# A chunked attention and a feed-forward block on one core: one list of calls, written in another order

## The chip, the core and the metric

The kernel runs on one core of a Trainium2 chip. Its time is the device time in microseconds of one execution. Five engines with instruction streams of their own take part: TensorE (PE; the loads of its weights are shown apart as PEld), VectorE (DVE), ScalarE (ACT), GpSimd (POOL) and SyncE (SP), which only issues transfers. The profile is one execution, recorded by the hardware profiler. An entry such as L388 names line 388 of the kernel's file, often a line inside a helper that is called from many places.

## The reference

First comes a causal linear attention with a decay per head, computed in blocks with a running state, then a feed-forward block on its output, token by token.

```python
# q, k, v: (B, H, S, D) = (4, 8, 768, 64), lam: one decay per head
Dmask = np.where(rel >= 0, lam[:, None, None] ** rel[None, :, :], 0.0)
for b in range(nb):
    intra = einsum('bhic,bhjc->bhij', qb, kb) * Dmask[None]
    intra = einsum('bhij,bhjd->bhid', intra, vb)
    inter = einsum('bhid,bhde->bhie', qb * lam_pow[None], kv_state)
    out[:, :, sl] = intra + inter
    kv_state = lam_block * kv_state + einsum('bhsd,bhse->bhde', kb * rev_pow, vb)
# x: the attention's output as 3072 tokens of 512; w_in: 512 x 2048, w_out: 2048 x 512
h = x @ w_in
g = np.maximum(h, 0.0) + alpha * np.minimum(h, 0.0)
return (g @ w_out).astype(np.float32)
```

The reference takes the attention in blocks of 64 rows. The kernel takes blocks of 128, which gives the same values with another mask and another power of the decay.

## The kernel before

**Units and chunks.** The 3072 tokens are six chunks of 512: chunk c holds the rows of sequence block c // 2 (256 rows) of two of the four batches. The attention of a chunk is four units, one per batch and half of the heads, 24 units in all, numbered n = 0 to 23. A unit has two score blocks of 128 rows for each of its four heads.

**Steps of a unit.** `load` brings q and k as fp32 (SyncE's queue, or GpSimd's with "G"), `load_v16` brings v and casts it to fp16 on the way (GpSimd's queue). `cast` (L245 to L251) makes q and k fp16, on ScalarE ("A"), VectorE ("V") or GpSimd ("G"); this letter stands behind many calls and means the same each time. `turn` transposes them on TensorE (L316) and `turn_copy` takes the result out of PSUM (L249 on VectorE, L247 on ScalarE); `turned` (L303) has a transfer do both. `decayed` multiplies q with its decay (L341). `score_products` (L377) makes the 128 x 1024 scores of a unit in PSUM, in the one buffer `s` that all units share. `masked` (L388, VectorE) multiplies them with the decay mask and frees that buffer. `inter` (L361) and `intra` (L402) add up the output, `attended` copies it to the chunk's `xT`. `key_decayed` (L290 on ScalarE in eight rows, otherwise L292) and `state_products` or `state_in` make the state's update, `states` (L457) and `first_state` write the new state `R`. The masks are made once at the start: `mask_logs` (L195, VectorE) writes the logarithms of the decay for two heads, `decay_mask` (L206, ScalarE) takes their exponential. `tick` (L145) runs products on TensorE whose result nobody reads.

**Steps of the feed-forward block.** `up` (L498) is h = x @ w_in for one of 16 blocks of 128 hidden columns. `relu` (L511, ScalarE) and `prelu` (L526, VectorE) make g from it. `down` and `down_copy` (L534, L548) are the second product of chunk 0 and its way out. `load_win` and `load_wout` bring the weights in four quarters each, cast by GpSimd's queue; `gate` (L115) makes SyncE's queue wait until a quarter is there.

**Seven products for eight.** The second product of chunks 1 to 5 runs as seven products of half the size in place of eight, on sums of weights (`w_sum`) and of values (`g_sum`): `second(c, i, b)` at L655 is one pass of eight products, `last` (L697) the seventh kind for chunk 5. The first product of chunks 4 and 5 is made together in the same manner (`in_sum`, `x_sum`, `first`, L780). All these sums are on VectorE or, with "G", on GpSimd, where L573 is a difference and L576 a sum. `g_sum(c, i, j, k)` overwrites quarters of chunk c's values for i = 2, 3 and 4, so that i = 4 needs i = 2 of the same j and k, which needs i = 1:

```python
if i == 1:
    add(s1, a21, a22, eng)
elif i == 3:
    sub(a21, a11, a21, eng)
elif i == 2:
    sub(a11, s1, a11, eng)
else:
    sub(a12, a12, a11, eng)
```

The pass with i = 5 reads the sum of i = 1, the pass with i = 6 that of i = 2, the pass with i = 7 the difference of i = 3, and the pass with i = 3 (`last` for chunk 5) that of i = 4; the passes with i = 1, 2 and 4 read values that are not yet, or not at all, overwritten.

**What sets the order.** The kernel runs under a manual schedule: each engine executes its instructions in the order in which the program lists the calls. From line 799 on the body is one list of some 1,080 calls, written out. Pools fix how far work can run ahead: four PSUM banks for transposes, projections and outputs, one score buffer, three `m` and three output buffers, five raw buffers for q and k.

**Ordered waits.** `vector_turn(n)` remembers the VectorE instruction listed last, and `gpsimd_waits(n)` makes the GpSimd instruction listed last wait until that one is done (L560, L563). No data passes between the two; the wait only says who goes first.

Of the kernel before, what the change touches and what calls it, by code (L numbers as in the profile page):

```python
# [11 lines left out]
def kernel(  # L12
# [469 lines left out]
    G = {}  # L482
# [315 lines left out]

    load(0, 1, "k", 0, "G")
    query_decay(3, 1)  # L800
    query_decay(2, 1)
    mask_logs(2)
    tick(6)
    load(0, 1, "q", 0, "G")
    mask_logs(0)
    key_decay()
    state_decay()
    load(0, 0, "k", None)
    cast(0, "k16", "V")
    query_decay(0, 1)  # L810
    load(0, 0, "q", None)
    key_decayed(0, "V")
    mask_logs(1)
    key_decayed(1, "V")
    decay_mask(2)
    decay_mask(0)
    cast(1, "k16", "V")
    tick(56)
    load(0, 1, "q", 1, "G")
    load_v16(1)  # L820
    decay_mask(1)
    cast(1, "q16", "A")
    mask_logs(3)
    query_decay(1, 1)
    cast(0, "q16", "V")
    vector_turn(0)
    turn(1, (1,))
    turn_copy(1, (1,), "V")
    decay_mask(3)
    query_decay(0, 0)  # L830
    load_alpha()
    load(0, 1, "k", 1, "G")
    load_v16(0)
    turn(1, (0,))
    turn_copy(1, (0,), "V")
    load_v16(2)
    turn(0, (1,))
    turn_copy(0, (1,), "V")
    turn(0, (0,))
    turn_copy(0, (0,), "A")  # L840
    load_v16(3)
    load_win(1)
    slopes_turn()
    slopes()
    load_win(0)
    decayed(1, "P")
    cast(2, "q16", "A")
    score_products(1)
    masked(1)
    fill(3)  # L850
    key_decayed(2)
    gpsimd_waits(0)
    cast(2, "k16", "A")
    cast(3, "q16", "G")
    gpsimd_waits(0)
    turn(2, (0,))
    turn_copy(2, (0,), "V")
    state_in(1, 0)
    first_state(1)
    decayed(2)  # L860
    decayed(0, "V")
    load_win(3)
    score_products(0)
    key_decayed(3)
    cast(3, "k16", "A")
    turn(2, (1,))
    load(1, 0, "k", 0, "G")
    inter(1)
    turn(3, (0,))
    state_in(0, 0)  # L870
    turn_copy(2, (1,), "A")
    first_state(0)
    intra(1)
    turn(3, (1,))
    attended(1, "A")
    masked(0)
    score_products(2)
    state_in(0, 1)
    inter(0)
    turn_copy(3, (0,), "V")  # L880
    decayed(3)
# [12 lines left out]
    first_state(3)
    masked(3)
    intra(2)
    state_in(3, 1)
    up(0, 4, 0)
    attended(2, "A")
    relu(0, 4, 0)  # L900
    state_in(2, 1)
    states(2, (1,))
    load_win(2)
    states(3, (1,))
    load(1, 1, "q", 1, "G")
    load(1, 0, "k", 1, "G")
    load(1, 0, "q", 1, "G")
    inter(3)
    prelu_half(0, 4, 0)
    intra(3)  # L910
    state_in(1, 1)
    attended(3, "A")
    up(0, 6)
    load_wout(0)
    up(0, 3)
    relu(0, 6)
    relu(0, 3)
    up(0, 5)
    states(1, (1,))
    cast(4, "q16", "G")  # L920
    prelu(0, 6)
    load(1, 1, "k", 1, "G")
    relu(0, 5)
    up(0, 7)
    relu(0, 7)
    load_wout(1)
    prelu(0, 3)
    cast(4, "k16", "G")
    up(0, 13)
    up(0, 15)  # L930
    load_v16(5)
    prelu(0, 5)
    relu(0, 13)
    prelu(0, 7)
    key_decayed(4)
    prelu(0, 13)
    cast(5, "k16", "G")
    cast(5, "q16", "G")
    up(0, 14)
    up(0, 1)  # L940
    relu(0, 15)
    prelu(0, 15)
    turn(4, (0,))
    load(1, 1, "q", 0, "G")
    load_wout(2)
    relu(0, 14)
    relu(0, 1)
    up(0, 0)
    prelu(0, 14)
    turn_copy(4, (0,), "V")  # L950
    up(0, 10)
    relu(0, 0)
    prelu(0, 1)
    turn(4, (1,))
    up(0, 2)
    cast(7, "q16", "A")
    prelu(0, 0)
    relu(0, 10)
    w_sum(1, 1, "G")
    in_sum(1, 2, "G")  # L960
    up(0, 9)
    turn_copy(4, (1,), "A")
    prelu(0, 10)
    up(0, 4, 1)
    relu(0, 2)
    gate(2, "out")
    up(0, 11)
    score_products(4)
    decayed(4, "V")
    query_decay(1, 0)  # L970
    relu(0, 9)
    load(1, 1, "k", 0)
    prelu(0, 2)
    relu(0, 4, 1)
    relu(0, 11)
    load_wout(3)
    state_products(4, None, True)
    prelu(0, 9)
    turn(5, (0,))
    up(0, 8)  # L980
    prelu_half(0, 4, 1)
    turn(7, (0,))
    prelu(0, 11)
    turn(5, (1,))
    turn_copy(5, (0,), "A")
    turn_copy(7, (0,), "V")
    load_v16(7)
    first_state(4)
    turn_copy(5, (1,), "A")
# [919 lines left out]
```

## Time and profile before

| | before |
|---|---|
| runs, us | 201.75, 205.83, 201.48 |
| median, us | 201.75 |
| profiled execution, us | 202.65 |
| its span, us | 200.9 |
| instructions | 5880 |
| TensorE busy, us (share) | 194.7 (97%) |
| VectorE busy, us (share) | 172.7 (86%) |
| ScalarE busy, us (share) | 135.6 (68%) |
| GpSimd busy, us (share) | 142.8 (71%) |
| moved by DMA | 30.53 MB |

The span runs from the first to the last instruction that the profile holds. The profiled execution took 1.75 us more than its span and 0.90 more than the median of the three runs. The ends of TensorE's products are modelled, so a row's end can lie past the start of the next; its starts are the safer reading. The page cuts the span into 40 slices and gives TensorE's granted clock in tenths of full speed, which is 9 ("90% or more") in all of them.

```profile
PE   7999999999999999999999999999999999999992
DVE  6998879987799998999998997999999999996600
ACT  5786778928886897787786692836768877632131
POOL 8999689997999749999799959967520505525300
PEclk9999999999999999999999999999999999999999
```

TensorE is full from the second slice to the last but one. VectorE comes near it in many slices between. GpSimd is full early and has holes from slice 28 on, which is where the first products of chunks 4 and 5 begin.

### The profile page before, as it was taken

The page shows a single profiled execution, that of the slowest core. Times are in us where ns is not written, and L with a number is a line of the kernel's source. Part 1 is how long each engine was busy: PE and PEld are TensorE (multiplying, and loading weights), DVE is VectorE, ACT ScalarE, POOL GpSimd, SP SyncE. Part 2 cuts the span into 40 slices and gives each one's busy share as a digit, 9 for nine tenths or more (in the row PEclk, how much of TensorE's full clock was granted, in tenths as well). Part 3 has the DMA queues.
Part 4 walks back from the last instruction along what each step waited for, and adds up shares of the span by engine and source line. Part 5 has one row for each costly group of instructions (what it writes and reads, how often), then busy time and mean ns, then how long its engine had stood idle before and what let it go on. Part 6 is the DMA issues. An engine that isn't in the chain of part 4 may idle for free.

```text
span 200.9 us, 5880 instructions
## 1 busy us (share of the span) xinstructions
PE 194.7 (97%) x2351; PEld 131.1 (65%) x2351; DVE 172.7 (86%) x319; ACT 135.6 (68%) x303; POOL 142.8 (71%) x161
## 2 busy tenths in 40 slices
PE   7999999999999999999999999999999999999992
PEld 7976445546545688665556777667666556788891
DVE  6998879987799998999998997999999999996600
ACT  5786778928886897787786692836768877632131
POOL 8999689997999749999799959967520505525300
PEclk9999999999999999999999999999999999999999
DMA  5999999999999699999999964011100003002343
GB/s 159 286 193 217 254 264 237 201 261 288 223 226 221 108 235 227 224 236 191 135 202 196 211 177 104 3 57 52 52 0 3 30 24 104 6 0 77 135 144 117
DMA packets 59199, 30.53 MB, mean 152 GB/s; under 512 B 29652, under 2 KB 57956, under 8 KB 59172
## 3 DMA queue, kind: packets, MB, share of 16 engines
q1 hardware_dynamic: 41236, 19.87, 42.6%
q0 software_dynamic: 17776, 10.23, 35.9%
q8 instruction: 18, 0.29, 0.6%
q14 instruction: 9, 0.07, 0.2%
q10 hardware_dynamic: 160, 0.07, 0.1%
HBM read 27.27 MB, written 6.29 MB: 167 GB/s over the span
## 4 chain that ended last, share of the span: by engine, by line
PE 58%; DMA 16%; POOL 10%; DVE 7%; issue 3%; ACT 3%; ACTq 0%; POOLq 0%
PE y L655 13%; PE h_ps L498 11%; PE b L655 10%; DMA v<-in_v_dram 7%; PE b L780 5%; DMA w_out_sb<-in_moe_w_out_dram 5%; DMA w_in_sb<-in_moe_w_in_dram 4%; PE e L780 3%; PE a L780 3%; POOL qdT L341 3%; PE o_ps L534 3%; PE unread L145 3%; DVE g L526 2%; POOL v L272 2%; DVE sm L388 2%
## 5 line engine op out<-in xcount | busy, mean ns | idle before, releaser
L498 PE MATMUL h_ps<-xT,w_in_sb 128*128 128x512 f16 (+1 forms) x264 | 59.5, 373 | 0.4 <-DMA w_in_sb<-in_moe_w_in_dram 0.3
L655 PEld LDWEIGHTS <-g 128*128 128x128 f16 x464 | 44.9, 98 | 10.4 <-issue 0.5
L526 DVE SCALAR_TENSOR_TENSOR g<-m,oma,h_ps 128x512 f16<-128x512 f32 (+1 forms) x66 | 46.2, 727 | 5.4 <-ACT m L511 4.2
L511 ACT ACTIVATE m<-h_ps 128x512 f32<-128x512 f32 (+1 forms) x66 | 37.8, 583 | 12.0 <-PE h_ps L498 11.4
L498 PEld LDWEIGHTS <-w_in_sb 128*128 128x128 f16 x264 | 24.4, 97 | 25.9 <-DMA w_in_sb<-in_moe_w_in_dram 1.0
L388 DVE TENSOR_TENSOR sm<-s,dmask 128x1024 f16<-128x1024 f32 x24 | 29.2, 1218 | 1.1 <-PE s L377 0.8
L655 PE MATMUL y<-w_out_sb,g 128*128 128x256 f16 x224 | 27.6, 273 | 0.2 <-DVE y L576 0.2
L341 POOL TENSOR_TENSOR qdT<-qkT,qdecay 128x512 f16<-128x512 f16 (+1 forms) x20 | 21.1, 1058 | 0.1
L290 ACT ACTIVATE kdec<-kraw,kdecay 128x64 f16<-128x64 f32 x80 | 20.1, 341 | 0.0
L247 ACT ACTIVATE xT<-acc 128x512 f16<-128x512 f32 x21 | 12.6, 598 | 11.0 <-DVE R L457 4.7
L655 PE MATMUL b<-t,g 128*128 128x256 f16 x160 | 19.3, 273 | 0.0
L573 POOL TENSOR_TENSOR g<-g,g 128x512 f16<-128x512 f16 x13 | 14.9, 1166 | 6.2 <-PE y L655 6.2
L272 POOL DMA_DIRECT2D v<-in_v_dram x24 | 18.8, 786 | 0.0
L457 DVE SCALAR_TENSOR_TENSOR R<-R,rdecay,acc 128x128 f16<-128x128 f16 x54 | 15.5, 341 | 1.0 <-ACT xT L247 0.4
L534 PE MATMUL o_ps<-w_out_sb,g 128*128 128x512 f16 x64 | 15.4, 380 | 0.0
L573 POOL TENSOR_TENSOR g<-g 128x512 f16<-128x512 f16 x8 | 9.2, 1155 | 8.6 <-DVE s L576 8.5
L292 POOL TENSOR_TENSOR kdec<-kraw,kdecay 128x512 f16<-128x512 f32 x12 | 12.7, 1057 | 0.2
L573 POOL TENSOR_TENSOR g<-s,g 128x512 f16<-128x512 f16 x5 | 6.1, 1225 | 5.8 <-DVE g L573 4.8
L377 PE MATMUL s<-qkT 64*64 64x128 f16 x384 | 9.9, 220 | 0.3 <-DVE qkT L249 0.2
L247 ACT ACTIVATE o_sb<-y 128x512 f32<-128x512 f32 (+2 forms) x12 | 6.3, 524 | 5.5 <-DMA out_dram<-o_sb 2.3
L576 POOL TENSOR_TENSOR w_in_sb<-g,g 128x512 f16<-128x512 f16 x3 | 3.5, 1159 | 9.1 <-PE a L780 9.1
L247 ACT ACTIVATE qk<-qraw 128x512 f16<-128x512 f32 x14 | 8.7, 625 | 1.7 <-DMA qraw<-in_q_dram 1.7
(131 smaller groups left out, 381.8 us busy)
## 6 DMA issues: line engine op xcount, KB each, us to landing
out_dram<-o_sb SPq DMA_DIRECT2D x23, 256.0 KB, 2.4
kraw<-in_k_dram SPq DMA_DIRECT2D x7, 512.0 KB, 5.6
qraw<-in_q_dram SPq DMA_DIRECT2D x6, 512.0 KB, 5.6
v<-in_v_dram POOLq DMA_DIRECT2D x24, 128.0 KB, 6.0
w_in_sb<-in_moe_w_in_dram POOLq DMA_DIRECT2D x4, 512.0 KB, 8.9
w_out_sb<-in_moe_w_out_dram POOLq DMA_DIRECT2D x4, 512.0 KB, 8.8
qraw<-in_q_dram POOLq DMA_DIRECT2D x6, 256.0 KB, 6.8
qraw<-in_q_dram SPq DMA_DIRECT2D x6, 256.0 KB, 6.0
```

The costliest lines, as they stand in the source:

```text
L247: nc.scalar.activation(out, in_, AF.Copy)
L272: nc.gpsimd.dma_start(out=v16.rearrange("p h e d -> p h (e d)"), in_=v[2 * (c % 2) + bi, ds(4 * hh, 4), ds((c // 2) * W, W), :].rearrange( ...
L290: nc.scalar.activation(kdec[:, e, h], kr[:, e, h], AF.Copy, scale=kdecay[:, x, e : e + 1])
L341: engine(eng).tensor_tensor(out=qdT[:, :, :, p], in0=(t["qps"] if eng == "P" else t["qkT"][:, 0])[:, :, :, p], in1=qdecay[:, hh, :, :, p], ...
L388: nc.vector.tensor_tensor(out=t["sm"].rearrange("p a h x j -> p (a h) x j"), in0=t["s"].rearrange("p a h x j -> p (a h) x j"), in1=mask_of ...
L498: nc.tensor.matmul(h[:, 0:n] if bi is None else h[:, 0:n].rearrange("p (e j) -> p e j", e=2), lhsT=w_in_sb[:, gi, ts(f, 128)], rhs=x.rearr ...
L511: nc.scalar.activation(m[:, 0:n], HP[c, f, bi][:, 0:n], AF.Relu, scale=-1.0)
L526: engine(eng).scalar_tensor_tensor(out=g, in0=m, scalar=oma[:, f : f + 1], in1=h, op0=ALU.mult, op1=ALU.add)
L534: nc.tensor.matmul(O[c, t], lhsT=g_of(c, f)[:, t // 2, t % 2, :], rhs=w_out_sb[:, f, :], start=(f == 0), stop=(f == NF - 1),)
L573: engine(eng).tensor_tensor(out=out, in0=a, in1=b, op=ALU.subtract)
L655: nc.tensor.matmul(Y[c, k][:, ds(b * HALF, HALF)], lhsT=left(c, i, f, b), rhs=right(i, f), start=(f == 0 and b == 0 and i in (1, 5)), stop ...
L780: nc.tensor.matmul(t, lhsT=w, rhs=x, start=(g == 0 and i in (1, 5)), stop=(g == 1), skip_group_check=True)
```

## The change

Nothing before line 799 is changed, and the helpers are the same to the letter. The list of calls from there on is written in another order, and some calls have another engine's letter. TensorE gets the same instructions, and the same transfers are issued. These counts of calls differ:

| call | before | after |
|---|---|---|
| `cast` of q or k on ScalarE, GpSimd, VectorE | 24, 18, 6 | 28, 17, 3 |
| `decayed` on GpSimd, on VectorE | 20, 4 | 23, 1 |
| `turn_copy` on ScalarE, on VectorE | 8, 9 | 5, 12 |
| `key_decayed` on ScalarE, VectorE, GpSimd | 10, 2, 12 | 9, 3, 12 |
| `g_sum` on GpSimd, on VectorE | 37, 43 | 43, 37 |
| `w_sum` on GpSimd, on VectorE | 7, 9 | 9, 7 |
| `vector_turn` | 13 | 16 |
| `gpsimd_waits` | 24 | 21 |

`tick(6)` and `tick(56)` both stood ahead of the first transposes; now `tick(56)` stands there and `tick(6)` behind them. The first loads of q and k on GpSimd's queue come in another order, and six such half blocks of chunk 1 stand ahead of w_out's first quarter, where five stood. `gate(2, "out")`, behind which SyncE's loads of later q and k wait, keeps its place in SyncE's queue. Of the last two chunks' 32 value sums GpSimd makes 20, before 12. The diff is nearly the whole list; this is its start, and its end from the last PReLU on.

```diff
--- before.py
+++ after.py
@@ -796,1082 +796,1082 @@
...
+    key_decay()
+    query_decay(1, 1)
+    load(0, 0, "k", None)
+    mask_logs(3)
+    tick(56)
+    mask_logs(1)
+    cast(0, "k16", "A")
+    cast(1, "k16", "A")
+    load(0, 1, "q", 0, "G")
+    load(0, 1, "q", 1, "G")
+    decay_mask(3)
+    mask_logs(2)
+    turn(0, (1,))
+    load_v16(1)
+    query_decay(3, 1)
+    key_decayed(0, "V")
     load(0, 1, "k", 0, "G")
-    query_decay(3, 1)
+    decay_mask(2)
+    turn(1, (1,))
+    load_v16(0)
+    turn_copy(0, (1,), "V")
+    load_v16(2)
+    load(0, 1, "k", 1, "G")
...
     prelu(5, 15)
-    g_sum(4, 3, 1, 0, "G")
-    second(4, 2, 0)
-    second_b(5)
-    second(4, 2, 1)
-    g_sum(4, 2, 0, 0)
-    second(4, 5, 0)
-    g_sum(5, 1, 1, 1)
-    g_sum(5, 1, 0, 1, "G")
-    second_store(3, 2)
-    second(4, 5, 1)
+    g_sum(4, 2, 0, 1)
+    g_sum(5, 1, 1, 1, "G")
     second(5, 2, 0)
+    second(5, 2, 1)
+    second_out(4, 2)
+    g_sum(4, 3, 1, 1)
+    vector_turn(11)
+    second_store(4, 2)
     second(5, 5, 0)
-    g_sum(5, 3, 1, 1)
-    g_sum(4, 2, 0, 1)
-    second_m5(4)
-    second(5, 5, 1)
-    g_sum(4, 2, 1, 0)
-    g_sum(5, 3, 0, 0)
-    g_sum(4, 3, 1, 1)
-    g_sum(5, 2, 1, 0)
-    second(5, 2, 1)
-    second_m5(5)
-    g_sum(5, 2, 1, 1, "G")
-    g_sum(5, 2, 0, 0)
-    g_sum(5, 4, 1, 0, "G")
     g_sum(4, 2, 1, 1)
     second(4, 6, 0)
-    g_sum(5, 3, 0, 1)
-    second_out(5, 2)
+    g_sum(5, 2, 0, 0, "G")
+    gpsimd_waits(11)
     g_sum(5, 2, 0, 1)
     vector_turn(12)
-    second_store(5, 2)
+    g_sum(5, 3, 1, 1, "G")
+    gpsimd_waits(12)
+    second(5, 5, 1)
+    second_store(3, 4)
     second(4, 6, 1)
+    g_sum(5, 2, 1, 0, "G")
+    g_sum(5, 2, 1, 1, "G")
+    second(5, 6, 0)
+    second_m5(4)
+    second(5, 6, 1)
     second_x(4)
-    second(5, 6, 0)
-    g_sum(4, 4, 0, 1, "G")
-    gpsimd_waits(12)
-    second(5, 6, 1)
+    g_sum(5, 4, 1, 1, "G")
     second(4, 7, 0)
+    g_sum(5, 4, 0, 1)
+    vector_turn(13)
+    second(4, 7, 1)
+    second_out(5, 2)
+    second_m5(5)
     second_x(5)
     g_sum(4, 4, 1, 0, "G")
-    g_sum(5, 4, 0, 1)
-    second(4, 7, 1)
-    g_sum(4, 4, 1, 1)
+    g_sum(5, 4, 0, 0, "G")
+    gpsimd_waits(13)
+    g_sum(5, 4, 1, 0)
+    vector_turn(14)
+    g_sum(4, 4, 0, 1, "G")
+    gpsimd_waits(14)
+    g_sum(4, 4, 0, 0)
+    vector_turn(15)
+    second_store(5, 2)
     second_out(4, 7)
-    g_sum(5, 4, 1, 1)
+    last(5, 0, 0, 256)
     second(5, 7, 0)
-    g_sum(4, 4, 0, 0)
     second(5, 7, 1)
+    last_copy(5, 0, 0, 256)
+    last(5, 1, 0, 128)
+    second_out(5, 7)
+    g_sum(4, 4, 1, 1, "G")
+    gpsimd_waits(15)
     second(4, 4, 0)
-    second_out(4, 2)
     second(4, 4, 1)
-    second_store(3, 4)
-    second_out(4, 4)
-    second_store(4, 2)
-    second_out(5, 7)
-    g_sum(5, 4, 0, 0, "G")
-    second_store(4, 7)
-    last(5, 0, 0, 256)
     second(4, 3, 0)
...
```

The first place is VectorE's queue in the opening, from the mask logarithms to the first mask. Here `rel_f`, `loglam` and `drop` make the logarithms, `qk_...` is a unit's fp16 q and k, `tp` a transpose in PSUM, `qkT` its copy, and L388 is a mask product. Before:

```order
L195 SCALAR_TENSOR_TENSOR dmask<-rel_f,loglam,drop 128x192 x4
L249 CAST qk_205<-kraw 128x512
L292 TENSOR_TENSOR kdec<-kraw,kdecay 128x512
L195 SCALAR_TENSOR_TENSOR dmask<-rel_f,loglam,drop 128x192 x2
L292 TENSOR_TENSOR kdec<-kraw,kdecay 128x512
L249 CAST qk_218<-kraw 128x512
L195 SCALAR_TENSOR_TENSOR dmask<-rel_f,loglam,drop 128x192 x2
L249 CAST qk_205<-qraw 128x512
L249 COPY qkT<-tp 128x512 x3
L237 TENSOR_SCALAR oma<-at_ps 128x16
L341 TENSOR_TENSOR qdT<-tp,qdecay 128x4x64
L388 TENSOR_TENSOR sm<-s,dmask 128x1024
```

And in the changed kernel:

```order
L195 SCALAR_TENSOR_TENSOR dmask<-rel_f,loglam,drop 128x192 x6
L292 TENSOR_TENSOR kdec<-kraw,kdecay 128x512
L249 COPY qkT<-tp 128x512
L292 TENSOR_TENSOR kdec<-kraw,kdecay 128x512
L249 CAST qk_251<-qraw 128x512
L195 SCALAR_TENSOR_TENSOR dmask<-rel_f,loglam,drop 128x192 x2
L249 COPY qkT<-tp 128x512
L341 TENSOR_TENSOR qdT<-tp,qdecay 128x4x64
L388 TENSOR_TENSOR sm<-s,dmask 128x1024
L249 COPY qkT<-tp 128x512
L388 TENSOR_TENSOR sm<-s,dmask 128x1024
L249 COPY qkT<-tp 128x512
```

Two key casts and a query cast left the queue for ScalarE. Behind the first copy of a transpose stand a key product, a query cast, two mask logarithms, a copy and a decay ahead of the first mask; the three copies that stood in a row are spread between the masks.

The second place is the end of GpSimd's queue, all in the last two chunks, up to the branch that ends the program. A `g_...` is a tile of four blocks of values, `w_in_sb` and `s_1507` hold the sums of i = 1 of chunk 5 and of chunk 4. Before, where `g_3231`, `g_3204`, `g_3414` and `g_3444` are chunk 5's:

```order
L576 TENSOR_TENSOR w_in_sb<-g_3231,g_3204 128x512
L576 TENSOR_TENSOR w_in_sb<-g_3414,g_3444 128x512
L576 TENSOR_TENSOR s_1507<-g_3395,g_3464 128x512
L576 TENSOR_TENSOR s_1507<-g_3147,g_3255 128x512
L573 TENSOR_TENSOR g_3395<-g_3395 128x2x256
L576 TENSOR_TENSOR w_in_sb<-g_3231,g_3204 128x512
L573 TENSOR_TENSOR g_3414<-w_in_sb,g_3414 128x2x256
L573 TENSOR_TENSOR g_3444<-g_3444,g_3414 128x2x256
L573 TENSOR_TENSOR g_3255<-g_3255,g_3147 128x2x256
L573 TENSOR_TENSOR g_3464<-g_3464,g_3395 128x2x256
L573 TENSOR_TENSOR g_3204<-g_3204,g_3231 128x2x256
```

And in the changed kernel, where `g_3188`, `g_3216`, `g_3411` and `g_3437` are chunk 5's:

```order
L573 TENSOR_TENSOR g_3166<-g_3166 128x2x256
L573 TENSOR_TENSOR g_3411<-g_3411 128x2x256
L573 TENSOR_TENSOR g_3382<-g_3382 128x2x256
L576 TENSOR_TENSOR w_in_sb<-g_3411,g_3437 128x512
L573 TENSOR_TENSOR g_3188<-w_in_sb,g_3188 128x2x256
L573 TENSOR_TENSOR g_3411<-g_3411 128x2x256
L573 TENSOR_TENSOR g_3411<-w_in_sb,g_3411 128x2x256 x2
L573 TENSOR_TENSOR g_3437<-g_3437,g_3411 128x2x256
L573 TENSOR_TENSOR g_3463<-g_3463,g_3382 128x2x256
L573 TENSOR_TENSOR g_3216<-g_3216,g_3188 128x2x256
L573 TENSOR_TENSOR g_3240<-g_3240,g_3166 128x2x256
L573 TENSOR_TENSOR g_3463<-g_3463,g_3382 128x2x256
```

The last L573 row before is `g_sum(5, 4, 0, 0)`, which `last(5, 0, 0, 256)` needs; the sum of chunk 5 that needs the last PReLU stood on VectorE. Now that sum is the row `w_in_sb<-g_3411,g_3437`, on GpSimd, and eight rows lead from it to the difference of `g_3216` and `g_3188`, which is `g_sum(5, 4, 0, 0)`.

More of the change, by code (lines that the diff above doesn't have):

```diff
@@ L1122 @@
     up(1, 0)
[L1123 to L1149 removed]
+    prelu(1, 6)
@@ L1524 @@
[L1524 to L1538 removed]
+    states(19, (0,))
+    g_sum(2, 2, 1, 1, "G")
+    second(2, 2, 1)
+    gate(1, "out")
+    turned(20)
+    relu(3, 13)
+    cast(23, "q16", "G")
+    g_sum(2, 2, 0, 0, "G")
+    relu(3, 7)
+    inter(19)
+    key_decayed(22, "A")
@@ new lines @@
+    score_products(20)
+    prelu(3, 13)
+    intra(19)
+    state_products(20)
+    attended(19, "A")
+    turned(21)
+    up(3, 14)
+    g_sum(2, 2, 1, 0)
+    vector_turn(5)
+    second_out(2, 2)
+    prelu(3, 7)
+    turned(22)
+    second(2, 6, 0)
+    decayed(20)
+    gpsimd_waits(5)
+    relu(3, 14)
+    key_decayed(23, "A")
+    g_sum(2, 4, 1, 0)
+    vector_turn(6)
+    in_sum(2, 2, "G")
+    gpsimd_waits(6)
+    states(20, (0,))
+    prelu(3, 14)
+    masked(20)
+    up(3, 11)
+    inter(20)
```

1537 lines of the change are left out of this document (741 added, 796 removed).

## The prediction

> **What bounds the kernel now.** I read the page first, then the busy time by stage, then TensorE in order of time.
>
> ```profile
> span 200.9 us, 5880 instructions
> ...
> PE 194.7 (97%) x2351; PEld 131.1 (65%) x2351; DVE 172.7 (86%) x319; ACT 135.6 (68%) x303; POOL 142.8 (71%) x161
> ```
>
> ```profile
> 0.00:20.00 20.00, 18.50 (x343) 15.11 (x344) 17.05 (x46) 13.85 (x31) 19.11 (x34) 1.00 1.12 213
> 20.00:30.00 10.00, 9.75 (x54) 4.65 (x53) 8.23 (x12) 7.19 (x14) 7.17 (x11) 1.00 1.20 260
> 30.00:60.00 30.00, 29.83 (x382) 16.03 (x380) 26.07 (x46) 22.94 (x63) 28.20 (x33) 1.00 1.23 240
> 60.00:100.00 40.00, 39.99 (x606) 26.83 (x605) 37.85 (x75) 32.63 (x79) 34.63 (x37) 1.00 1.20 197
> 100.00:140.00 40.00, 39.52 (x538) 26.73 (x538) 37.58 (x64) 26.39 (x59) 34.02 (x32) 1.00 0.75 128
> 140.00:172.00 32.00, 32.00 (x204) 19.67 (x203) 31.17 (x52) 23.51 (x43) 12.37 (x12) 1.00 0.10 34
> 172.00:195.00 23.00, 23.00 (x214) 20.27 (x212) 14.79 (x30) 7.75 (x16) 7.31 (x7) 1.00 0.22 76
> 195.00:201.00 6.00, 2.09 (x24) 1.76 (x21) 0.00 (x0) 1.35 (x3) 0.00 (x0) 1.00 0.31 109
> ```
>
> Behind each stretch stand its length and the busy time of PE, PEld, DVE, ACT and POOL. From 20 to 195 us TensorE is idle for 0.25 + 0.17 + 0.01 + 0.48 = 0.91 us, so it sets the time there. VectorE has 2.15 us to spare in the 40 us from 60 on, 2.42 in the next 40 and 0.83 in the 32 after them: it is nearly a second bound. GpSimd has 23.00 - 7.31 = 15.7 us free at the end. So what counts is where TensorE's dense work begins, what holds it up after that, and what is left behind its last product.
>
> ```profile
> 13.57 0.42 PE L377 MATMUL s<-qkT 64*64 64x128 f16 x16
> ...
> 18.25 7.12 PE L498 MATMUL h_ps<-xT,w_in_sb 128*128 128x512 f16 x32
> ...
> 25.43 1.03 PE L498 MATMUL h_ps<-xT,w_in_sb 128*128 128x512 f16 x4
> 26.71 1.04 PE L498 MATMUL h_ps<-xT,w_in_sb 128*128 128x512 f16 x4 [0.25 <-DMA w_in_sb<-in_moe_w_in_dram]
> ...
> 33.81 1.89 PE L534 MATMUL o_ps<-w_out_sb,g 128*128 128x512 f16 x8
> ```
>
> Dense work begins at 18.25. The ends of products are modelled and overlap the next: 32 of them in some 7 us are 0.22 us each. Four from 25.43 on are thus over at 26.30, and the next four start at 26.71. That is 0.41 us lost to the weights, more than the 0.25 shown. Such hidden gaps come on top of the 0.91 us.
>
> **The opening: +0.8 us.** TensorE gets to dense work through four mask products (L388). They share one score buffer, so each waits for the one before.
>
> ```profile
> 5.08 0.42 DVE L249 CAST qk<-kraw 128x512 f16<-128x512 f32 x1
> ...
> 6.01 0.74 DVE L195 SCALAR_TENSOR_TENSOR dmask<-rel_f,loglam,drop 128x192 f32<-128x192 f32 x2
> 6.67 0.68 DVE L292 TENSOR_TENSOR kdec<-kraw,kdecay 128x512 f16<-128x512 f32 x1
> ...
> 8.26 0.42 DVE L249 CAST qk<-qraw 128x512 f16<-128x512 f32 x1
> 8.90 1.09 DVE L249 COPY qkT<-tp 128x512 f16<-128x512 f16 x3 [0.22 <-PE tp L316]
> ...
> 9.98 0.41 DVE L341 TENSOR_TENSOR qdT<-tp,qdecay 128x256 f16<-128x256 f16 x1
> 10.31 1.22 DVE L388 TENSOR_TENSOR sm<-s,dmask 128x1024 f16<-128x1024 f32 x1
> ...
> 14.03 1.22 DVE L388 TENSOR_TENSOR sm<-s,dmask 128x1024 f16<-128x1024 f32 x1 [0.19 <-PE s L377]
> 15.17 0.59 DVE L457 SCALAR_TENSOR_TENSOR R<-R,rdecay,kv 128x128 f16<-128x128 f16 x2
> 15.77 1.22 DVE L388 TENSOR_TENSOR sm<-s,dmask 128x1024 f16<-128x1024 f32 x1
> ```
>
> Key casts go to ScalarE and the keys are turned first; key 0 had landed by 5.08. But behind its first copy of a turned key VectorE now has a key product (0.68), a query cast (0.42), two mask logs (0.74), a copy (1.09 / 3 = 0.36) and a decay (0.41) before the first mask. That is 2.6 us, about 2.4 with the overlap of 0.06 to 0.09 that the starts show. The first copy can start at about 8.6, a little before the 8.90 above, since six ticks fewer stand ahead of the transposes. With its own 0.36 the first mask starts at 11.35, 1.05 later than 10.31. The three steps to the last were 15.77 - 10.31 = 5.46 us. Now the first two are bound by the score buffer: mask 1.22, then from score to mask 14.03 - 13.57 = 0.46, and some 0.05 between engines, so 1.73 each. The third also gets two state rows (0.59), about 2.1. Together 5.56, and the last mask starts at 16.9, 1.15 late. From it to dense work were 18.25 - 15.77 = 2.48 us; the last unit's products come closer behind it now, and I count 2.15. That leaves +0.8. It is 0 if the VectorE chain overlaps better than here, and 1.4 if neither the steps nor the last stretch shorten.
>
> **Loads and first projections: -0.4 us.** The projection that waited at 26.71 for the last quarter of w_in now has a half block and a full block more ahead of it: 1.3 us, against 0.41 lost. That wait goes. Late next would be w_out, with one 256 KB load more ahead of it.
>
> ```profile
> 21.92 9.62 DMA w_out_sb<-in_moe_w_out_dram
> ```
>
> This piece of the chain ends at 31.54. At 240 GB/s (the stretch from 30 on) the load takes 1.1 us, so w_out's first quarter lands at 32.6, and its first use was at 33.81: covered by 1.2 us, and without that cover it costs what it is late. Range -0.4 to +0.3. The loads of q and k by SyncE keep their place behind the gate on w_out.
>
> **The middle, 30 to 172: -0.2 us.** Three decays and three casts leave VectorE; three copies and one key product come to it. ScalarE has four casts more, three copies and one key product (eight rows) fewer. Eight sums move from VectorE to GpSimd.
>
> ```profile
> L573 POOL TENSOR_TENSOR g<-g,g 128x512 f16<-128x512 f16 x13 | 14.9, 1166 | 6.2 <-PE y L655 6.2
> ...
> L576 DVE TENSOR_TENSOR s<-g,g 128x512 f16<-128x512 f16 x9 | 6.5, 739 | 0.0
> ...
> L573 DVE TENSOR_TENSOR g<-s,g 128x512 f16<-128x512 f16 x11 | 5.3, 502 | 0.0
> ```
>
> VectorE loses 8 sums of 0.50 to 0.74, 4.0 to 5.9 us of 172.7; GpSimd gains 8 x 1.17 = 9.3 on 142.8. Neither can bind the whole. A gain is bounded by TensorE's 0.91 us and hidden gaps, which I put at -1.5 in all; as every wait here is made anew, I take the same size the other way, +1.5. The value is small, and a gain, since VectorE was the short engine.
>
> **The end: +0.4 us.** In the last two chunks GpSimd takes 20 of the 32 sums, before 12, and `last(5, 0, 0, 256)` moves ahead of four passes of TensorE.
>
> ```profile
> 171.89 2.78 PE L655 MATMUL y<-w_out_sb,g 128*128 128x256 f16 x24
> ...
> 182.94 3.66 PE L655 MATMUL b<-t,g 128*128 128x256 f16 x32
> 186.43 3.66 PE L655 MATMUL b<-w_out_sb,g 128*128 128x256 f16 x32
> ```
>
> ```profile
> 177.24 0.74 DVE L526 SCALAR_TENSOR_TENSOR g<-m,oma,d 128x512 f16<-128x512 f32 x1
> ```
>
> A pass of eight products is (186.43 - 182.94) / 4 = 0.87 us. Counted from 171.89, the start of `second(4, 1, 0)`, the product named comes after 18 passes and two products of 0.22: at 16.1. The last PReLU (the row at 177.24) ended 6.1 after that start; with one 0.42 sum more before it, 6.5. Only then can GpSimd begin `g_sum(5, 1, 1, 1)`, and eight of its sums in a row lead to `g_sum(5, 4, 0, 0)`, which that product needs: 6.5 + 8 x 1.17 = 15.9. No wait, by 0.2 us. But three of the ordered waits put VectorE sums of 0.42 between them: 17.1, 1.0 late. I take 0.4 from 0 to 1.0, and up to 1.9 if one of these sums has to wait for GpSimd, as here:
>
> ```profile
> 37.30 1.27 DVE L573 TENSOR_TENSOR t<-w_out_sb 128x512 f16<-128x512 f16 x1
> ```
>
> ```profile
> 37.13 1.15 POOL L576 TENSOR_TENSOR s<-w_in_sb 128x512 f16<-128x512 f16 x1
> ```
>
> ```profile
> 182.01 0.41 DVE L573 TENSOR_TENSOR g<-s,g 128x512 f16<-128x512 f16 x1
> ```
>
> A VectorE sum takes 0.41 alone and 1.27 when a GpSimd sum runs: it ends 0.29 after that one, 0.86 dearer. The Trainium skill, page SBUF — State Buffer, section Who interferes with whom, says that a VectorE instruction with two SBUF inputs and a GpSimd one that reads SBUF exclude each other for the whole instruction, whichever begins first. By that rule the end costs 1.9, the sum is +2.1 and the time 203.9; the trace agrees with it at 37.30.
>
> The drain after the last product keeps its copy and store.
>
> **The sum.** 0.8 - 0.4 - 0.2 + 0.4 = +0.6 us. The profiled execution took 202.65 (span 200.9 and 1.75 around it), 0.9 over the median of 201.75. I add to the median and round up: 202.4.
>
> **Rivals.** *VectorE starves early (slower).* Between the query cast of unit 3 and the key product of unit 8 no GpSimd wait is left, where ten stood, and VectorE has eight weight sums there. If each meets a GpSimd sum it pays 0.86: 6.9 us, against 30.00 - 26.07 = 3.9 to spare from 30 to 60. The 3.0 over that hold up masks and copies; two casts and a key product of the same unit, if they meet too, add 0.86 twice. With 4.7 lost the forecast becomes 207.1. It decides from the fifth meeting on. For it: GpSimd is busy for 28.20 of those 30 us. Against: DMA issues lie between its sums. Chance 0.12.
>
> *The new order fills the gaps (faster).* The 0.91 us and three hidden gaps of 0.41 go, and the opening costs nothing: 201.75 - 2.1 = 199.6. For it: the two fullest engines of the middle are relieved. Against: the walk of the opening. Chance 0.30, and 0.03 of it for the 4.0 us that pass 2%, which is more than the trace has to give.
>
> *It moves nothing:* TensorE's work is the same and the other engines hide the rest, so 201.75 within half a microsecond. Chance 0.18.
>
> The forecast with its terms' spread has 0.40.
>
> **Range and chances.** The low end is the second rival, 199.6. The high end: the forecast with the upper bounds of the opening (+0.6), the end (+1.5) and the middle (+1.7) is 206.2; they will hardly come together, so 205.6. The first rival is left outside, and little of the second. Faster or slower by over 2%, 4.0 us, is about what a measurement of this kernel can tell from no change: slower has the first rival's 0.12, faster 0.03, and the rest is 0.85.
>
> **What would show it.** Right: the first mask at 11.3 and dense projections from 19.1; no wait for w_in; TensorE waiting before its first L697 row while GpSimd runs without a pause. Wrong: dense work by 18.3; VectorE sums of 1.2 us by the handful between 30 and 60 and TensorE idle there for over 2 us (the first rival); no idle time at all past 20 us (the second).

## The result and the profile after

| | before | changed |
|---|---|---|
| runs | 9 | 9 |
| median, us | 201.54 | 202.99 |
| lowest and highest, us | 201.31, 206.37 | 202.49, 204.01 |
| profiled execution, us (span) | 202.65 (200.9) | 202.76 (201.0) |

The ratio is 1.0072, with a 95% interval from 1.0048 to 1.0097: the changed kernel is 1.45 us slower by the medians, and within 2%. Before's 205.83 and 206.37 are executions in a slower state, which the interval leaves out. The forecast was 202.4, 0.65 us over the median then known.

The two profiled executions differ by 0.11 us only, so the loss cannot be read from that pair: before's was 1.1 us over its median. One more profile of the same kernel (the run `before_again` below) took 201.34 us with a span of 199.6. It is the ordinary one (the twelve runs of it have the median 201.67), and the changed kernel is compared with it from here on. Their spans differ by 1.4 us, as the medians do. First the busy time by stage, changed kernel, columns as in the prediction:

```profile
30.00:60.00 30.00, 30.00 (x369) 16.09 (x367) 25.06 (x46) 19.89 (x49) 26.02 (x30) 1.00 1.21 229
...
140.00:172.00 32.00, 31.55 (x196) 19.15 (x197) 30.74 (x47) 24.11 (x45) 18.30 (x17) 1.00 0.12 42
172.00:195.00 23.00, 22.38 (x207) 19.60 (x206) 13.97 (x22) 7.13 (x14) 13.98 (x12) 1.00 0.20 69
```

And of the ordinary execution of before, the same two late stages:

```profile
140.00:172.00 32.00, 32.00 (x204) 19.77 (x203) 31.09 (x52) 24.61 (x45) 12.37 (x12) 1.00 0.10 34
172.00:195.00 23.00, 23.00 (x214) 20.25 (x212) 13.55 (x28) 7.22 (x14) 5.97 (x6) 1.00 0.22 78
```

TensorE was full in both stages and now is not, while GpSimd works 6 and 8 us more there. TensorE in order of time shows two places in the changed kernel:

```profile
139.21 0.59 PE L780 MATMUL a<-xT,w_in_sb 128*128 128x512 f16 x2
140.45 0.61 PE L780 MATMUL b<-xT,w_in_sb 128*128 128x512 f16 x2 [0.65 <-DVE e L576]
141.04 1.02 PE L780 MATMUL e<-xT,s 128*128 128x512 f16 x4
...
185.79 1.91 PE L655 MATMUL b<-w_out_sb,g 128*128 128x256 f16 x16
188.32 1.05 PE L697 MATMUL y<-w_out_sb,g 128*128 128x256 f16 x8 [0.62 <-POOL g L573]
```

Two products from 139.21 on need 0.43 us at the rate of this stage and the next begins 1.24 later: 0.81 lost, and another 0.15 between 140.45 and 141.04 (0.59 for 0.43). Sixteen half-width ones from 185.79 on need 1.74, so 0.78 is lost at 188.32 (0.15 and 0.78 come from unrounded starts). Sum 1.74. In the ordinary execution of before the same counting finds 0.16 at 26.3 (the wait for w_in) and 0.25 at the place below. There the starts leave 0.35, of which 0.09 stand at the same place in the changed kernel too:

```profile
42.20 1.67 PE L534 MATMUL o_ps<-w_out_sb,g 128*128 128x512 f16 x7
44.06 0.42 PE L377 MATMUL s<-qkT 64*64 64x128 f16 x16 [0.18 <-DVE qkT L249]
```

So 1.74 - 0.41 = 1.33 of the 1.4 us are these waits, and 0.1 is left for the opening. Who is late at 140.45 is VectorE. The adds of `first_x` (L576, `e`) stand in its queue behind a row of twelve sums, which it works through from 135.49 on with hardly a pause, while GpSimd idles for 4.96 us until one of these sums is there. The end of the row on VectorE, and then GpSimd of the changed kernel:

```profile
139.37 0.42 DVE L573 TENSOR_TENSOR w_in_sb<-w_in_sb 128x512 f16<-128x512 f16 x1
139.71 1.29 DVE L576 TENSOR_TENSOR e<-b,m 128x512 f32<-128x512 f32 x2
```

```profile
133.48 1.15 POOL L573 TENSOR_TENSOR xT<-xT 128x512 f16<-128x512 f16 x1 [1.86 <-ACT xT L247]
139.59 1.20 POOL L573 TENSOR_TENSOR g<-s,g 128x512 f16<-128x512 f16 x1 [4.96 <-DVE g L573]
```

At the end GpSimd's chain is late, along the steps that the prediction had listed:

```profile
177.82 1.54 POOL L576 TENSOR_TENSOR w_in_sb<-g,g 128x512 f16<-128x512 f16 x1 [4.19 <-DVE g L526]
179.32 1.33 POOL L573 TENSOR_TENSOR g<-w_in_sb,g 128x512 f16<-128x512 f16 x1
181.08 1.15 POOL L573 TENSOR_TENSOR g<-g 128x512 f16<-128x512 f16 x1 [0.42 <-DVE g L573]
182.19 2.26 POOL L573 TENSOR_TENSOR g<-w_in_sb,g 128x512 f16<-128x512 f16 x2
184.53 6.15 POOL L573 TENSOR_TENSOR g<-g,g 128x512 f16<-128x512 f16 x5
```

The eighth sum is the third of the last row and ends at 188.27; the product that needs it starts at 188.32. One ordered wait costs 0.42, and the dear sums (1.54, 1.33) are those with a VectorE sum beside them.

### The profile page after: what moved, and what is told of

It is laid out like the page before. It is cut to its first block, busy times and chain, and to the rows that moved or that the text cites. A ratio compares the mean times of both kernels' runs of the same rounds, so it can differ in the third digit from the quotient of the medians.

```text
span 201.0 us, 5883 instructions
## 1 busy us (share of the span) xinstructions
PE 193.1 (96%) x2351; PEld 129.3 (64%) x2351; DVE 169.9 (85%) x309; ACT 133.3 (66%) x296; POOL 154.1 (77%) x171
## 5 line engine op out<-in xcount | busy, mean ns | idle before, releaser
L511 ACT ACTIVATE m<-h_ps 128x512 f32<-128x512 f32 (+1 forms) x66 | 36.7, 584 | 14.5 <-PE h_ps L498 13.7
L388 DVE TENSOR_TENSOR sm<-s,dmask 128x1024 f16<-128x1024 f32 x24 | 29.2, 1217 | 2.0 <-PE s L377 1.8
L655 PE MATMUL y<-w_out_sb,g 128*128 128x256 f16 x224 | 27.1, 273 | 0.0
L341 POOL TENSOR_TENSOR qdT<-qkT,qdecay 128x512 f16<-128x512 f16 (+1 forms) x23 | 23.7, 1038 | 2.8 <-DVE qkT L249 2.0
L655 PE MATMUL b<-t,g 128*128 128x256 f16 x160 | 19.9, 273 | 0.0
L290 ACT ACTIVATE kdec<-kraw,kdecay 128x64 f16<-128x64 f32 x72 | 18.0, 341 | 0.0
L576 POOL TENSOR_TENSOR s<-g,g 128x512 f16<-128x512 f16 x10 | 11.4, 1151 | 5.9 <-DVE g L526 5.9
L573 POOL TENSOR_TENSOR g<-g,g 128x512 f16<-128x512 f16 x12 | 14.1, 1198 | 2.3 <-DVE g L526 1.3
L573 POOL TENSOR_TENSOR g<-s,g 128x512 f16<-128x512 f16 x5 | 5.9, 1174 | 9.5 <-DVE g L573 9.5
L573 POOL TENSOR_TENSOR g<-g 128x512 f16<-128x512 f16 x10 | 11.4, 1154 | 1.1 <-DVE g L526 0.7
L576 POOL TENSOR_TENSOR w_in_sb<-g,g 128x512 f16<-128x512 f16 x3 | 3.9, 1285 | 9.0 <-DVE g L526 9.0
```

The source lines that it names most:

```text
L290: nc.scalar.activation(kdec[:, e, h], kr[:, e, h], AF.Copy, scale=kdecay[:, x, e : e + 1])
L341: engine(eng).tensor_tensor(out=qdT[:, :, :, p], in0=(t["qps"] if eng == "P" else t["qkT"][:, 0])[:, :, :, p], in1=qdecay[:, hh, :, :, p], ...
L388: nc.vector.tensor_tensor(out=t["sm"].rearrange("p a h x j -> p (a h) x j"), in0=t["s"].rearrange("p a h x j -> p (a h) x j"), in1=mask_of ...
L511: nc.scalar.activation(m[:, 0:n], HP[c, f, bi][:, 0:n], AF.Relu, scale=-1.0)
L573: engine(eng).tensor_tensor(out=out, in0=a, in1=b, op=ALU.subtract)
L576: engine(eng).tensor_tensor(out=out, in0=a, in1=b, op=ALU.add)
```

## The experiments

My theory from these traces: the loss is two new waits, at the first products of chunks 4 and 5 and at the end, and the opening costs next to nothing. The rivals: the opening costs 0.8 as forecast; or the middle as a whole is slower.

**One part of the list at a time.** The lists hold the same 1,043 calls, apart from the ordered waits and some engine letters, so a kernel can follow one list to a point and take the remaining calls in the order of the other. The edits, in this order for the opening, the middle and the end alone, each against before:

```diff
-    load(0, 1, "k", 0, "G")
...
-    attended(3, "A")
+    key_decay()
...
+    attended(3, "A")
```

```diff
     attended(3, "A")
-    up(0, 6)
-    load_wout(0)
...
+    query_decay(2, 0)
+    load(1, 1, "q", 0, "G")
...
+    second(4, 1, 0)
```

```diff
     second(4, 1, 0)
-    g_sum(4, 1, 1, 0, "G")
...
+    g_sum(5, 3, 0, 0, "G")
...
+    g_sum(5, 1, 1, 1, "G")
...
+    last(5, 0, 0, 256)
```

> The changed list up to attended(3, "A"), so to the end of the first four units, and then the list of before. By the forecast's terms the opening costs +0.8 us (0 to 1.4) against before. By the two traces laid side by side (the first mask 10.70 against 10.31, the last 16.02 against 15.77, the first projection after the last attention product 17.94 against 18.25) it costs 0.0 to 0.3 us. By the rival that the loss lies in the middle it costs nothing.

> Before's first four units, then the changed list up to second(4, 1, 0), then before's end. By the forecast's terms -0.4 (loads) -0.2 (middle) = -0.6 us. By the traces: gaps of TensorE of 0.42, 0.24, 0.28, 0.20 and 0.41 us gone, a new one of 0.81 at 139.43, so -0.7 us. By the rival that the whole loss sits in the middle and only ordinary executions of before show it: +1 or more.

> Before's list up to second(4, 1, 0), then the changed end. By the forecast's term +0.4 us (0 to 1.0, up to 1.9 with sums that wait for one another). By the trace of the changed kernel, where TensorE waits 0.78 us at 187.43 for GpSimd's chain of eight, +0.8. If only the opening or the middle matters: 0.

> The kernel before once more, to see which of its traces is the ordinary one. Its profiled execution took 202.65 us (span 200.9), 1.1 over the median of its runs, 201.54. If that execution was unlucky, this one has a span of about 199.8 and lacks some of the gaps (the 0.42 us at 26.08, the sums that wait for GpSimd at 37.30, 114.19, 136.94 or 179.36). If profiling itself costs 1.1 us, the span is 200.9 again with the same gaps. Ratio 1.000.

Measured: the opening alone 1.012 of before (1.0076 to 1.0163), the middle alone 1.0091 (1.0061 to 1.012), the end alone 1.0091 (1.0058 to 1.0124), and before again 0.9986 (0.9963 to 1.0009). The three parts cost 6 us together, the whole change 1.45: they do not add up, since each joint makes waits that neither list has. TensorE of the opening alone, ahead of unit 4, and of the middle alone, in two places:

```profile
27.67 1.89 PE L498 MATMUL h_ps<-xT,w_in_sb 128*128 128x512 f16 x8
31.53 2.43 PE L498 MATMUL h_ps<-xT,w_in_sb 128*128 128x256 f16 x8 [1.97 <-ACT qkT L247]
```

```profile
29.81 0.40 PE L316 MATMUL tp<-ident,qk 128*128 128x128 f16 x4 [0.90 <-POOL qk L251]
...
142.51 0.61 PE L780 MATMUL b<-xT,w_in_sb 128*128 128x512 f16 x2 [0.65 <-DVE e L576]
```

The 1.97 and the 0.90 are such joints, and the end alone has one of 1.06 at 177.77. The execution profiled for the opening alone took 205.69, the longest of its six, and there the wait brought a second loss: TensorE's granted clock was 0.50 from 32 to 35 us, and its full-width products started 427 ns apart, where 216 is usual. But the wait for `e` comes with the middle and at its old size, and the wait for GpSimd's chain comes with the end alone:

```profile
187.50 1.91 PE L655 MATMUL b<-w_out_sb,g 128*128 128x256 f16 x16
190.02 1.05 PE L697 MATMUL y<-w_out_sb,g 128*128 128x256 f16 x8 [0.61 <-POOL g L573]
```

So the times of these three decide nothing on the terms; their traces place each of the two waits in its part.

**The wait at the end.** `last` was moved by two passes, and then by one. (From here on the kernels also swap the numbers 7 and 8 of two ordered waits that hold back the same GpSimd instruction; who waits for whom stays the same.)

```diff
-    last(5, 0, 0, 256)
     second(5, 7, 0)
     second(5, 7, 1)
+    last(5, 0, 0, 256)
     last_copy(5, 0, 0, 256)
     last(5, 1, 0, 128)
```

> The changed kernel with one call moved: last(5, 0, 0, 256) stands behind second(5, 7, 1) and no longer ahead of second(5, 7, 0). If TensorE's 0.78 us at 187.43 is a wait for GpSimd's chain and nothing else, two passes of 0.87 us cover it: 0.8 us less than the changed kernel, so 202.2 us, 0.6 over before. If the chain also holds up what follows, or the wait moves to second(4, 4, 0), no gain: 203.0.

It took 202.79 us, 1.0049 of before (1.0022 to 1.0077) and 0.2 less than the changed kernel. The wait for GpSimd was gone, and another had come, 0.64 by the starts:

```profile
190.54 1.04 PE L697 MATMUL y<-w_out_sb,g 128*128 128x256 f16 x8
192.05 0.61 PE L697 MATMUL y<-w_out_sb,g 128*128 128x128 f16 x8 [0.47 <-ACT o_sb L247]
```

The two `last` calls write the same PSUM tile, and the copy of the first one's part stands between them. The passes had covered that copy.

```diff
-    last(5, 0, 0, 256)
     second(5, 7, 0)
+    last(5, 0, 0, 256)
     second(5, 7, 1)
```

> The changed kernel with last(5, 0, 0, 256) moved by one pass, between second(5, 7, 0) and second(5, 7, 1). One pass (0.87 us) covers TensorE's wait for GpSimd's chain (0.78), and the other lies between this call and last(5, 1, 0, 128), which had to wait 0.64 for ScalarE's copy when the two stood together. If the end's loss is this one wait: 0.8 us less than the changed kernel, so 202.2. If the two calls' copies are late anyway: 202.8 as with both passes ahead.

202.64 us, 1.0023 of before (0.9993 to 1.0052), and neither wait in the trace. The last product begins 0.89 earlier than in the changed kernel (195.75 against 196.64), 0.10 of it from the opening. That is the 0.8 expected. The median shows 0.35 of it, since the twelve times lie in two groups of six: the lower one, 201.85 to 202.34, is about 0.8 under the lower seven of the changed kernel's nine, 202.49 to 203.20. The ticks below are the likely reason for the groups.

**The row of sums.** The edit moves four of VectorE's sums behind `first_x`:

```diff
-    g_sum(3, 1, 1, 1)
...
-    g_sum(3, 3, 1, 1)
...
-    g_sum(3, 2, 1, 1)
...
-    g_sum(3, 3, 0, 0)
...
     first_x(0)
     first_x(1)
+    g_sum(3, 1, 1, 1)
+    g_sum(3, 3, 1, 1)
+    g_sum(3, 2, 1, 1)
+    g_sum(3, 3, 0, 0)
     first(0, 7)
```

> The changed kernel with four VectorE sums of chunk 3 (g_sum(3, 1, 1, 1), g_sum(3, 3, 1, 1), g_sum(3, 2, 1, 1), g_sum(3, 3, 0, 0)) moved from ahead of first_x(0) and first_x(1) to right behind them. If the waits of TensorE at 139.43 and 140.68 (0.81 and 0.15) come from VectorE reaching first_x late behind its row of sums, four sums of 0.34 take them away: 0.9 us less than the changed kernel, so 202.1, 0.5 over before. If ScalarE's first_m5 is late anyway, or the moved sums are late for second(3, ...), nothing or half of it.

> Both moves in the changed kernel. If the two waits are the whole loss, 1.7 us less than the changed kernel: 201.3, level with before or 0.3 under it, since before keeps gaps of 0.16 and 0.25 us in the middle that the changed kernel has not. If the opening costs 0.8 as forecast, 202.0 or more stays.

A miss: 204.11 us (1.0131 of before, 1.0093 to 1.0169), and 204.00 with `last` moved too. The wait for `first_x` is gone, and four others of 2.25 us in all have come, the largest 1.32 by the starts. The trace of the first of the two is from an execution of 205.57, well over its median, but that of the second, at 203.90, has the same four waits to within 0.01. TensorE and GpSimd of the first:

```profile
143.30 0.59 PE L780 MATMUL a<-xT,w_in_sb 128*128 128x512 f16 x2 [0.25 <-DVE g L526]
145.05 0.59 PE L780 MATMUL b<-x,w_in_sb 128*128 128x512 f16 x2 [1.16 <-POOL x L573]
```

```profile
142.73 1.16 POOL L573 TENSOR_TENSOR g<-s,g 128x512 f16<-128x512 f16 x1 [6.58 <-PE e L780]
143.84 1.16 POOL L573 TENSOR_TENSOR x<-xT,x 128x512 f16<-128x512 f16 x1
```

GpSimd's next sum, `g_sum(3, 2, 0, 0)`, overwrites what the last of the moved ones reads, so it has to wait for that one, which ended at 142.59 (the row names PE, whose product was long done). The `x` that TensorE waits for stands behind it in GpSimd's queue. PReLUs became late too (the 0.25). The sums were in the way of `first_x`, but they could not simply go later.

**Without the ordered waits.**

```diff
-    gpsimd_waits(0)
...
-    gpsimd_waits(15)
```

> The changed kernel without its 21 ordered waits. If these keep GpSimd's sums off VectorE's, VectorE sums of 0.8 to 1.4 us grow from the nine of the changed kernel's trace to over fifteen, and where VectorE is full (100 to 172) TensorE waits: +0.5 to +2 us. By the rival that they only delay GpSimd, its chain at the end starts 0.4 us earlier, TensorE's wait at 187.43 shrinks to 0.4, and the time falls by 0.4 us.

211.89 us, 1.0496 of before (1.0467 to 1.0525). Most of it is one place, at 77 us; VectorE and GpSimd there:

```profile
75.77 8.73 DVE L573 TENSOR_TENSOR g<-g,g 128x512 f16<-128x512 f16 x2
```

```profile
77.14 1.17 POOL L573 TENSOR_TENSOR g<-g,g 128x512 f16<-128x512 f16 x1
78.26 1.16 POOL L341 TENSOR_TENSOR qdT<-qkT,qdecay 128x512 f16<-128x512 f16 x1
79.37 1.04 POOL L292 TENSOR_TENSOR kdec<-kraw,kdecay 128x512 f16<-128x512 f32 x1
80.38 1.15 POOL L341 TENSOR_TENSOR qdT<-qkT,qdecay 128x512 f16<-128x512 f16 x1
81.49 2.25 POOL L573 TENSOR_TENSOR t<-w_out_sb,t 128x512 f16<-128x512 f16 x2
83.69 0.80 POOL L272 DMA_DIRECT2D v<-in_v_dram  x1
```

Two VectorE sums that took 1.21 us in the changed kernel take 8.73. The second begins at 76.58 and does not end while six GpSimd instructions run that read two tiles of SBUF each and follow one another without a pause. TensorE waits 7.27 us behind it, and 1.5 more go right after: behind the long wait its granted clock is 0.50 (the last figure but two below), and its half-width products start 213 ns apart, where 109 is usual:

```profile
86.00:87.00 1.00, 1.00 (x6) 0.70 (x5) 1.00 (x2) 0.78 (x2) 1.00 (x2) 0.50 0.70 68
```

Both expectations were wrong on the number: it is not more sums at 0.8 to 1.4 us each (eight over 0.9, where the changed kernel has nine), but one sum behind a whole run. The sum that waited is `g_sum(1, 4, 0, 1)`, for which `gpsimd_waits(3)` makes GpSimd hold back `g_sum(1, 4, 1, 1)`. That this one wait prevents the loss is read from the trace; it was not taken out alone. The wait at the end was 0.32 here, so there the rival had it right.

**The ticks.**

```diff
-    tick(56)
+    tick(24)
```

> The changed kernel with tick(24) in place of tick(56) ahead of the first transposes; the products left out are read by nobody. In its traces 37 to 53 of these products take 107 ns each before they take 56, and the first transposes start when they are over, at 6.97 to 8.35 us, though ScalarE has cast the first keys by 6.1. If the count of ticks holds up the opening, the first transposes start at about 6.0, the spread between executions shrinks, and 0.7 to 1.5 us are gained: 201.5 to 202.3. If TensorE reaches 56 ns only after so much work, the transposes and score products run at the slower rate and nothing is gained, or up to 1 us lost.

> Both edits in the changed kernel. If they add up, 200.7 to 201.5, under before by 0 to 0.8 us; if the loads of w_in bound the first projections once the opening is shorter (quarter 2 landed at 26.2 and was used at about 27.5), only 1.3 us of it in all.

The start of the transposes is where executions of one kernel differ. Products of `tick` per stretch of 1 us, with TensorE's granted clock as the last figure but two, in the changed kernel and, below it, in `f_last`, whose opening is the same list:

```profile
4.30:5.30 1.00, 1.00 (x12) 1.00 (x10) 1.00 1.16 296
5.30:6.30 1.00, 1.00 (x19) 1.00 (x17) 1.00 1.21 320
6.30:7.30 1.00, 1.00 (x21) 1.00 (x19) 1.00 1.02 287
```

```profile
5.30:6.30 1.00, 1.00 (x13) 1.00 (x11) 1.00 1.24 328
6.30:7.30 1.00, 1.00 (x17) 1.00 (x16) 1.00 0.98 274
```

The starts lie 107 ns apart, then 56, and the change came at 5.5 us in the one and at 6.7 in the other. Over all traces with 56 of these products it came between 4.5 and 7.5. In the traces with the changed opening 12 to 39 of the 56 took 107 ns (the 37 to 53 above are too many). The transposes, which stand behind the ticks, began at 7.42 and 8.00, and the dense projections at 17.94 and 19.19. Of these 1.25 us the ticks explain 0.6, which is what the first mask is late as well. The rest is a stop of TensorE in `f_last` behind the first of sixteen products, with nothing that the profile shows it waiting for:

```profile
16.18 0.41 PE L402 MATMUL acc<-sm,v 64*64 64x128 f16 x15 [0.46 <-issue]
```

All three traces with the changed opening and a late change (6.6 to 7.5) have this stop, and none with an early one has it; why is open. The twelve times of `f_last` lie in two groups, 202.49 to 202.79 and 203.57 to 203.87. That the moment of the change makes the groups fits the traces (`f_last`, `f_first`: late and from the upper group; the changed kernel, `f_both`, `g_last`: early and from the lower), but no run sets that moment. Either way, medians of a few runs hide 0.8 us.

With 24 ticks the transposes began at 5.68 and the first mask at 9.54 instead of 10.70, but the projections at 17.47, only 0.47 earlier: the state products now waited 0.59 for v (DMA), and later ones 0.22 and 0.15 for GpSimd's key products and casts. In the trace of `h_best` below the 24 products were over before the change, so that its first transposes still started 107 ns apart; its first mask came at 9.44 all the same. The time was 202.62 us (1.0030 of before, 1.0011 to 1.0049) and the spread of twelve runs 0.8 us, before it 1.5 with nine. So the count of ticks does hold up the opening. The gain is smaller than the 0.7 to 1.5 expected by the medians, 0.37, and at its low end by the ratios to before measured beside each, 0.42% or 0.85 us. With `last` moved by one pass as well it took 202.58 us (1.0039, 1.0017 to 1.0061). I had expected 200.7 to 201.5, so the two gains did not add up. The last product ends at 196.08, 1.17 before that of the changed kernel; the profile's last event follows it by 4.23 us, where it was 3.72 in the changed kernel. ScalarE's copies at the end show why. All of them write the three output buffers, and one had to wait longer for a store to leave its buffer; the changed kernel, then this one:

```profile
191.78 0.28 ACT L247 ACTIVATE o_sb<-y 128x128 f32<-128x128 f32 x1 [1.99 <-DMA out_dram<-o_sb]
```

```profile
193.05 0.28 ACT L247 ACTIVATE o_sb<-y 128x128 f32<-128x128 f32 x1 [3.56 <-DMA out_dram<-o_sb]
```

The copies behind it followed late, the last one ending 1.02 us after TensorE, where it was 0.37. Why that store took longer in the three kernels with 24 ticks is open.

**All three places.** Of the row of sums, two (`in_sum`) are needed only for blocks 4 to 7 of the first product. They go to GpSimd, into two pauses behind the row:

```diff
-    in_sum(4, 1)
...
-    in_sum(3, 1)
...
     g_sum(3, 4, 0, 1, "G")
+    in_sum(4, 1, "G")
...
     g_sum(3, 4, 1, 1, "G")
+    in_sum(3, 1, "G")
```

> The changed kernel with tick(24), with last(5, 0, 0, 256) between the two passes of second(5, 7, ...), and with two sums of VectorE's row ahead of first_x(0), in_sum(4, 1) and in_sum(3, 1), which only blocks 4 to 7 of the first product need, put on GpSimd into its pauses of 1.33 and 0.69 us at 148.4 and 152.0. VectorE comes to first_x(0) and first_x(1) 0.68 us earlier, and unlike the four sums that were only pushed back, these two leave it. If VectorE's row is what TensorE waits for at 139.4, its wait of 0.81 shrinks to 0.13 and that of 0.15 goes: 0.8 us under the kernel with the other two edits (202.58), so 201.8 and level with before (201.76). If GpSimd's added sums hold up VectorE's one sum there or GpSimd's own later chain, the wait only moves: 202.6.

202.20 us, 1.0013 of before (0.9995 to 1.0030; before measured beside it took 202.19). TensorE there:

```profile
138.81 0.59 PE L780 MATMUL a<-xT,w_in_sb 128*128 128x512 f16 x2
139.38 0.60 PE L780 MATMUL b<-xT,w_in_sb 128*128 128x512 f16 x2
139.97 1.02 PE L780 MATMUL e<-xT,s 128*128 128x512 f16 x4
```

0.57 for two products of 0.43, where it was 1.24: the wait shrank from 0.81 to 0.14, as expected (the 0.15 behind it stayed). Of the 0.8 us expected, 0.4 show in the median. The last product ends at 195.59, 0.18 before that of the ordinary execution of before, but the last event follows 4.47 us later, where it was 3.78, and again a copy had waited for its buffer, 3.81 us. With the three places mended the changed order is level with before. It does not beat it. Before itself was not run with 24 ticks, so a part of the level may be the ticks alone; against it, before's two traces have their transposes at 8.47 and 7.74 and their dense work at 18.25 and 18.28, so there the ticks did not set it.

## Why the prediction came out as it did

The range and the direction held, in part by luck: the opening was put 0.7 us too high and the middle 0.9 too low, and the two largely cancel. The forecast was +0.65 us by four terms, the result +1.45; sorted by the trace of the ordinary execution of before:

- **The opening, +0.8:** 0.1 in the profiled execution, 1.25 more in `f_last`, where TensorE's rate changes late. The failed step is "the first copy can start at about 8.6". The keys cast by ScalarE were ready by 6.2, and the copy waited for the ticks alone: 7.84, or 8.42 in `f_last`. The steps between masks were sized right in this execution (5.32 us for the three, against 5.56); in `f_last` they took 6.00, with the stop of TensorE in them. VectorE of the changed kernel, the first copy, the first mask and the last:

```profile
7.84 0.42 DVE L249 COPY qkT<-tp 128x512 f16<-128x512 f16 x1 [1.45 <-PE tp L316]
...
10.70 1.22 DVE L388 TENSOR_TENSOR sm<-s,dmask 128x1024 f16<-128x1024 f32 x1 [0.16 <-PE s L377]
...
16.02 1.22 DVE L388 TENSOR_TENSOR sm<-s,dmask 128x1024 f16<-128x1024 f32 x1
```

   The start of dense work was a poor mark: the 18.25 of before came behind four half-width projections, 0.44 us of work that the changed list does later. The 19.1 of the prediction is near the late case, 19.19, but by luck: it had no stop of TensorE in its sum.
- **The loads, -0.4:** the mechanism held, w_out's first quarter landed at 32.24 (predicted 32.6), 1.3 us ahead of its use. The size was off: the ordinary execution of before loses 0.16 at w_in, not 0.41.
- **The middle, -0.2 within 1.5 either way:** +0.7, from 0.25 gone at 44.06 and 0.96 new at 140. The step that failed is "a gain, since VectorE was the short engine". VectorE's total fell, 172.7 to 169.9, but a local row of sums ahead of `first_x` did the damage. It could be seen in the order of the calls, and I had walked only the opening and the end.
- **The end, +0.4 from 0 to 1.0:** 0.78, by the chain that was named. Counted from `second(4, 1, 0)` at 171.38, it began 6.4 us after (predicted 6.5), its last sum ended at 16.9 (15.9 without waits, 17.1 with), and TensorE was there at 16.2 (16.1). The size 0.4 was a choice between none and 1.0.

The rival in which VectorE starves early did not come true: TensorE is busy for 30.00 of 30 us from 30 to 60. Its mechanism is real and was priced far too low, at 0.86 per meeting; without the ordered waits a single meeting cost 7.3 us. The Trainium skill, page SBUF — State Buffer, section Who interferes with whom, says that the one that issues first holds the shared ports for its whole instruction. The trace agrees for one instruction, at 37.30. In the run without the ordered waits the sum's record begins 0.56 us before the first of the six instructions, so going first did not help it there; that it is held through six in a row, the page does not say. The rival that the gaps fill came half true: between 20 and 139 us the changed kernel has no gap over 0.15 us left, and lost more elsewhere. The rival that nothing moves, within half a microsecond, did not hold: the interval puts the loss at 1.0 to 2.0 us.

## What to carry to other kernels

Compare profiles that stand at their kernels' medians: one execution 1.1 us over the median hid the whole result. When an order is changed on engines that are nearly full, look for the place where one engine's row of deferrable work stands ahead of what the fullest engine needs next, and check what else in the second queue hangs on each piece before moving it. Where VectorE and GpSimd both read two SBUF tiles, a pause in GpSimd's queue at the right place was worth over 7 us here by the trace, though the wait itself does no work. And when the fullest engine gets done earlier, look at what drains behind it: here the wait for one of three output buffers took back part of what had been won.

## What the hardware showed that I had not expected

- TensorE's products of 128 columns start 107 ns apart at first and 56 ns apart later, and the profile's granted clock is 1.00 in both stretches. Whoever looks for the slower rate there must count starts. The Trainium skill, page TensorE: Matmul & The Clock Gate, Part 1, gives 106.7 and 55.6 ns for the two rates and says that the change comes with a window that does not start with the kernel. The traces agree on the rates, and the moment moved between 4.5 and 7.5 us from one execution to the next.
- A wait of TensorE can cost more than itself. Behind waits of 2.1 us (the opening alone) and 7.3 us (no ordered waits) the granted clock was 0.50, and TensorE worked at half its rate for some 3.4 us; behind waits of 1.1 us (the middle alone) and 1.3 us (`f_first`) it did not.
- A VectorE sum with two SBUF inputs took 7.9 us, once, while GpSimd instructions ran in a row. It ended with the issue of a transfer (83.69, 0.80 long). An issue of the same kind from 76.33 to 77.12 had not released it, and why is open.
